# A head's row maxima: from a seven-row product on VectorE to one row by ScalarE and a DMA, with new ranks for the planner

## The chip, the cores and the metric

The kernel runs on one core of one Trainium2 chip. The metric is the device time of one execution in microseconds; several runs are taken and their median is given. A profiled execution of the same program gives the trace that is read here.

## The reference

Three layers follow one another. The first is causal attention with decay, for 4 batches of 8 heads, 576 positions, 64 columns a head. The other two are feed-forward layers on the 2304 tokens that come out of it, 512 columns wide.

```python
# attention, per batch and head; q, k, v: 576 x 64, f: 576
scores = q @ k.T / sqrt(64)
cum = cumsum(log(clip(f, 1e-4, 1)))
scores = where(causal, -1e9, scores + cum[:, None] - cum[None, :])
scores = scores - max(scores, axis=-1)
attn = exp(scores) / (sum(exp(scores)) + 1e-9)
x = attn @ v                                   # heads side by side: 2304 x 512
# second layer
x = ((x @ w_a) * (x @ w_b)) @ w_out            # 512 -> 1536 -> 512
# third layer
h = x @ w_in                                   # 512 -> 1024
s = h * softmax(h)
out = ((s - mean(s)) / sqrt(var(s) + 1e-6) * g_ln) @ w_out2    # 1024 -> 512
```

All tensors are float32 in HBM. The weights w_a, w_b, w_out, w_in and w_out2 are converted on the way in (`load_cols`), from 8-byte words.

## The kernel before, in words

**The planner.** The kernel does not issue instructions directly. Each piece of work is an `op` with an engine (or several to choose from), a rank (`key`), a cost in us, and the buffers it reads and writes. `Sched.run` then plays the whole program through once, when the kernel is built: at each step the engine and operation that could start first is taken, and among those of one engine that could start within `WIN` = 0.02 us of it the one with the lowest rank. The result is one fixed order of instructions for each engine. The dictionary `Y` holds the numbers from which ranks are made. The planner's costs stand in `t_act`, `t_dve`, `t_pool1`, `t_pool2` and `t_mm`; a DMA is done when earlier ones have passed at 230 GB/s, plus 2.0 us (lines 244 to 246):

```python
            if e == "SP":
                dma_free = max(dma_free, t + dur) + o.nbytes / 230.0e3
                done = dma_free + 2.0
```

All DMAs are issued by one queue, SP. Up to rank 210, where the plan leaves TensorE idle for more than 0.3 us, 70% of that gap is filled with small matmuls whose result nobody reads (line 1503, the filler).

**Precision.** A float32 matrix product is made of three products of reduced-precision parts: each operand has a high part (a cast) and a low part (the rest, a subtraction). That is why casts on ScalarE and subtractions on GpSimd or VectorE are everywhere.

**The attention.** A list of 40 jobs is worked off: the first half of 8 heads of batch 0 (256 positions, kind K0), their second half (320 positions, kind K1), and 24 whole heads (kind KF). Job j has the rank `Z[j]`: it starts at `Z0` and grows by `T0` for K0, `T1` for K1, `TA` for the first 8 KF heads and `TF` for the other 16. For each head: keys and queries are transposed on TensorE (`turn`, line 763) and split (`split_k`, `split_q`), a copy of each high part is moved to other partitions by a DMA (lines 776 and 790), and the running sums of log f come by DMA as two more rows (`load_cum`). Three sets of such buffers exist. Then follows:

- `max_scores`: a coarse product (line 820) whose row maxima VectorE takes tile by tile (lines 839 and 842). They stand in the columns of `mt`, 128 positions to a column; TensorE transposes that into PSUM (line 851), so that each of up to five rows holds the maxima of 128 positions.
- the spread: these maxima have to be subtracted inside the product of the scores. VectorE multiplies the transposed rows with a 0/1 mask, `bmask`, and writes seven rows of the buffer `MB` (line 863); for some K0 heads ScalarE does it instead, in two pieces (line 868). Against rows of -1 in `SB` the product then subtracts each maximum.
- `scores`: two products to a piece (lines 886 and 894); the second has 64 + 7 rows and contains sums and maxima.
- `exps`: the exponential on ScalarE (line 936), for KF heads the causal mask on GpSimd (945), the split into parts (952 and 958).
- `v_split` (972, 977), `weigh` (992) and `out_`: the product with v, and the division.

**The first product of the second layer.** After each half of a batch, `split_x` (1064, 1068) prepares its columns and 12 units follow (`up_unit`): 24 matmuls each (line 1082), one for each block of 128 columns of w_a and w_b. Their rank is `UK` above that of the unit. ScalarE and VectorE take the result (1101, 1103) and a DMA puts it into HBM. The columns of w_a and w_b are loaded and converted by `load_cols` (fetch at 594; 609, 618, 627, 629, 633; cast at 646; subtraction at 651), with ranks from `W0`, `WD0` and `WD1`. The batch-0 units need K0 heads (first half) or K1 heads (second half), and their weight columns.

**The rest.** w_out, w_in and w_out2 are loaded in the same way, into buffers that the attention no longer needs. `down` (1333) makes the second product of layer two, `expert` the third layer (1386 to 1476).

The functions that the change touches, and what calls them:

Of the kernel before, what the change touches and what calls it, by code (L numbers as in the profile page):

```python
# [24 lines left out]
def t_act(n, psum=False):  # L25
    return (0.155 if psum else 0.187) + n / 1200.0
# [41 lines left out]
class Sched:  # L68
# [223 lines left out]
    "WD0": 0.382,  # L292
    "WN": 4,
    "WD1": 4.394,
# [15 lines left out]
    "RA": 1,  # L310
    "TB": 1,
    "MM": 1,
    "MX": -0.17,
    "XK": -0.753,
# [5 lines left out]
def kernel(  # L320
# [16 lines left out]
    P = 128  # L337
# [40 lines left out]
    sml = pool.tile([P, 40], F32, name="sml")  # L378
# [177 lines left out]
    def load_cols(src_view, key, dst_hi, dst_lo, wbuf, wparts, tfetch=6.0, scale=None, kind=1,  # L556
                  after=(), places=False):
# [83 lines left out]

        def shaped(dst):
# [168 lines left out]
    def max_scores(t, st, K, key):  # L811

        ms = [s_.buf("att", bank_att(K.mb[i])) for i in range(len(K.mm))]

        def mm(part):
            for o, w, i, k0 in K.mm[part]:
                d0 = o + i * P - k0
                dw = min(P, o + w - d0)
                pm = K.pm and Y["MM"] and o <= d0 < o + w
# [8 lines left out]
        for part in range(len(K.mm)):  # L828
            more = [P for x in K.mm[part] if K.pm and Y["MM"] and x[3] <= x[2] * P < x[3] + x[1]]
            op((PE, t_mm([x[1] for x in K.mm[part]] + more)), key + 0.1 * part,  # L830
               lambda part=part: mm(part), r=[(CONST, "cmask"), (CONST, "identb"), (st, "kh"), (st, "qh"), (st, "cum0"), (st, "cum1"), (st, "rows")],
               w=[(ms[part], i) for _, _, i, _ in K.mm[part]])

        def red(part, o, w, i):
# [3 lines left out]
            if K.pm and Y["MM"]:  # L838
                nc.vector.tensor_reduce(
                    out=mt(st)[:n, 2 + i:3 + i], in_=x, op=ALU.max, axis=AX.X)  # L840
                return
            nc.vector.tensor_tensor_reduce(  # L842
                out=x, in0=x, in1=cmask[:n, off:off + w], scale=1.0, scalar=-3.0e38,
                op0=ALU.add, op1=ALU.max, accum_out=mt(st)[:n, 2 + i:3 + i])

        for j, (part, o, w, i) in enumerate(K.red):
            op(("DVE", t_dve(w) + (0.0 if K.pm and Y["MM"] else 0.14)), key + Y["MX"] + 0.3 + 0.3 * j,
# [23 lines left out]
        rw.fn = spread  # L871

    def scores(t, st, K, key):
# [4 lines left out]
        def mm(i, last):  # L878
            for c, pi, o, q0, q1 in K.pieces:
# [83 lines left out]
    def v_split(nb, K, key):  # L963
# [4 lines left out]
        def vv(part):  # L968
# [85 lines left out]
    def split_x(i, key):  # L1054
# [5 lines left out]
        for p in range(NP):  # L1060
# [3 lines left out]
            op(("ACT", t_act(n)), key + 0.3 * p, lambda p=p, s=src: nc.scalar.copy(  # L1064
                out=xsv(h, 0, n)[:, p], in_=s()), r=rd, w=[(xh, p)], after=AX1 if i == 1 else ())
# [486 lines left out]
```

## Time and profile before

| | us |
|---|---|
| median of 3 runs | 951.99 |
| lowest, highest | 948.39, 953.69 |
| the profiled execution, its time | 949.74 |
| the profiled execution, its span in the trace | 947.7 |
| TensorE busy | 916.3 |
| VectorE busy | 598.1 |
| ScalarE busy | 460.2 |
| GpSimd busy | 189.3 |

In the rows below, PE is TensorE, PEld its weight loads, DVE VectorE, ACT ScalarE, POOL GpSimd, and SP the queue that issues the DMAs. L863 is line 863 of the kernel. A group of instructions is given as line, engine, operation, output and input; then busy us and mean ns of one; then the idle time just before them and what ended it. A share or a sum of busy time is an average over stages with different limits, so the stages are to be read one by one. The filler counts as busy.

### The profile page before, as it was taken

The numbers are of one execution on the slowest core, as the hardware profiler recorded it, in microseconds if no ns is written. First come the engines' busy times: TensorE is split into PE (matmuls) and PEld (weight loads), VectorE is DVE, ScalarE is ACT, GpSimd is POOL, SyncE is SP. The second block draws the span as 40 slices with busy tenths as digits, with TensorE's granted clock in tenths as the row PEclk, the third lists the DMA queues.
The fourth block names the chain that finished last, engine by engine and source line by source line (L and its number), as shares of the span: only waits on it lengthen the run. The fifth ranks groups of instructions, "written<-read, shape, count | busy, mean of one in ns | idle before, by whom it ended". The sixth has DMA issues, their size and how long they took to land.

```text
span 947.7 us, 16069 instructions
## 1 busy us (share of the span) xinstructions
PE 916.3 (97%) x5888; PEld 835.8 (88%) x5888; DVE 598.1 (63%) x1162; ACT 460.2 (49%) x862; POOL 189.3 (20%) x280
## 2 busy tenths in 40 slices
PE   6789998999999999999999999999999999999997
PEld 5678997999999999999999889988888888888885
DVE  6799988777577766577454957744543444444553
ACT  3897877666555645445445645522322322232222
POOL 4122323444341332211211001110100010010100
PEclk8999999999999999999999999999999999999999
DMA  4656545334133423233226545412212121111000
GB/s 120 189 151 187 143 124 130 93 86 101 41 97 88 106 59 77 58 94 82 78 84 224 196 131 180 130 45 56 57 55 65 47 56 45 40 45 34 25 15 33
DMA packets 124001, 86.89 MB, mean 92 GB/s; under 512 B 74346, under 2 KB 114292, under 8 KB 123924
## 3 DMA queue, kind: packets, MB, share of 16 engines
q1 hardware_dynamic: 123924, 85.88, 32.3%
q8 instruction: 46, 0.75, 0.3%
q14 instruction: 31, 0.25, 0.1%
HBM read 56.86 MB, written 19.02 MB: 80 GB/s over the span
## 4 chain that ended last, share of the span: by engine, by line
PE 81%; DVE 2%; ACT 1%; issue 0%; POOL 0%; DVEq 0%; ACTq 0%
PE ps L1082 29%; PE ps L1333 16%; PE ps L1386 10%; PE ps L1463 10%; PE ps L992 7%; PE ps L894 2%; PE ps L820 2%; PE ps L886 2%; PE ps L1448 2%; PE ps L763 1%; DVE ps L842 0%; PE ps L851 0%; ACT pfw L936 0%; ACT pexp L952 0%; DVE wms L629 0%
## 5 line engine op out<-in xcount | busy, mean ns | idle before, releaser
L1082 PE MATMUL ps<-xs,wt 128*128 128x288 f32 (+2 forms) x2304 | 332.0, 298 | 0.6 <-ACT ats L1101 0.5
L1082 PEld LDWEIGHTS ps<-xs,wt 128*128 128x128 f32 x2304 | 312.9, 188 | 2.6 <-ACT ats L1101 0.7
L992 PE MATMUL ps<-pexp,VS 128*128 128x64 f32 (+5 forms) x600 | 96.8, 303 | 6.4 <-ACT pexp L952 3.3
L992 PEld LDWEIGHTS ps<-pexp,VS 128*128 128x128 f32 x600 | 90.5, 189 | 11.5 <-DVE pexp L958 3.5
L1463 PE MATMUL ps<-wt 128*128 128x512 f32 x408 | 98.2, 390 | 0.0
L1101 ACT COPY ats<-ps 128x288 f32<-128x288 f32 (+2 forms) x96 | 38.3, 399 | 117.4 <-PE ps L1082 113.8
L1333 PE MATMUL ps<-wt,sets 128*128 128x512 f32 (+1 forms) x420 | 92.7, 370 | 0.0
L1463 PEld LDWEIGHTS ps<-wt 128*128 128x128 f32 x408 | 76.0, 188 | 15.4
L1333 PEld LDWEIGHTS ps<-wt,sets 128*128 128x128 f32 x420 | 73.1, 188 | 12.9
L1325 POOL TENSOR_TENSOR wt<-nat,wt 128x512 fp32r<-128x512 f32 (+1 forms) x26 | 27.4, 1054 | 251.1 <-ACT wt L1321 251.1
L842 DVE CUSTOM_DVE_ANT_0 ps<-ps,cmask 128x512 f32<-128x512 f32 (+4 forms) x120 | 64.6, 551 | 11.5 <-PE ps L820 8.6
L1103 DVE TENSOR_TENSOR gts<-ps,ats 128x288 f32<-128x288 f32 (+2 forms) x84 | 38.3, 456 | 47.7 <-PE ps L1082 21.0
L945 POOL TENSOR_SCALAR_AFFINE_SELECT pfw<-pfw 128x128 f32<-128x128 f32 (+1 forms) x120 | 38.8, 351 | 139.4 <-ACT pfw L936 138.5
L1321 ACT CAST wt<-nat 128x512 fp32r<-128x512 f32 (+1 forms) x60 | 34.7, 579 | 55.1 <-PE ps L1333 26.4
L1386 PE MATMUL ps<-wt 128*128 128x512 f32 x240 | 57.8, 394 | 0.7 <-DVE wt L1346 0.7
L1403 ACT ACTIVATE xrw<-ps,sml 128x1024 f32<-128x1024 f32 x17 | 19.0, 1118 | 79.3 <-DVE sml L1401 79.3
L1454 DVE TENSOR_TENSOR wt<-ps,wt 128x512 fp32r<-128x512 f32 x34 | 23.3, 689 | 53.3 <-ACT wt L1451 53.3
L1401 DVE TENSOR_REDUCE sml<-ps 128x1 f32<-128x1024 f32 x18 | 22.0, 1225 | 49.2 <-PE ps L1386 49.2
L1386 PEld LDWEIGHTS ps<-wt 128*128 128x128 f32 x240 | 44.2, 188 | 9.9 <-DVE wt L1346 1.2
L894 PE MATMUL ps<-sets 71*128 71x448 f32 (+4 forms) x200 | 51.2, 332 | 0.0
L958 DVE TENSOR_TENSOR pexp<-pfw,pexp 128x960 fp32r<-128x960 f32 (+1 forms) x40 | 41.2, 1042 | 14.9 <-ACT pexp L952 14.8
L886 PE MATMUL ps<-sets 128*128 128x64 f32 (+5 forms) x200 | 49.7, 294 | 0.6 <-ACT pfw L936 0.5
(161 smaller groups left out, 1531.3 us busy)
## 6 DMA issues: line engine op xcount, KB each, us to landing
gs<-gts SPq DMA_DIRECT2D x60, 144.0 KB
sets<-sets SPq DMA_DIRECT2D x56, 144.0 KB
nat<-gs SPq DMA_DIRECT2D x36, 144.0 KB
raws<-in_moe_w_a_dram SPq DMA_DIRECT2D x10, 512.0 KB
pfw<-in_moe_w_b_dram SPq DMA_DIRECT2D x10, 512.0 KB
nat<-gs SPq DMA_DIRECT2D x36, 128.0 KB
out_dram<-xrw SPq DMA_DIRECT2D x18, 256.0 KB
nat<-in_k_dram SPq DMA_DIRECT2D x32, 128.0 KB
```

The source lines that it names most:

```text
L842: nc.vector.tensor_tensor_reduce(out=x, in0=x, in1=cmask[:n, off:off + w], scale=1.0, scalar=-3.0e38, op0=ALU.add, op1=ALU.max, accum_out= ...
L886: nc.tensor.matmul(dst, lhsT=SA(st)[:, ks], rhs=MA(st)[:, q0:q1], start=True, stop=False)
L894: nc.tensor.matmul(dst, lhsT=SB(st)[:D + NA, ks], rhs=MB(st)[:D + NA, q0:q1], start=False, stop=True)
L945: nc.gpsimd.affine_select(out=x, in_=x, pattern=[[1, w]], base=0, channel_multiplier=-1, compare_op=ALU.is_ge, fill=0.0)
L958: o.fn = lambda o=o, bh=bh, bl=bl, n=n, pf=pf: ENG[o.eng].tensor_tensor(out=pexp[:, 64 * bl.slot:64 * bl.slot + n], in0=pf(), in1=pexp[:, ...
L992: nc.tensor.matmul(bank(u, K.uo + q0, q1 - q0), lhsT=V[:, vp], rhs=src[:, o:o + q1 - q0], start=(k_ in K.first and ip == 0), stop=(k_ in K ...
L1082: nc.tensor.matmul(bank(u[m], 0, n_), lhsT=wv(m, wp, c)[:, kk], rhs=xsv(h, xx, n_)[:, kk], start=(n == 0), stop=(n == 3 * KD - 1))
L1101: op(("ACT", t_act(n_, True)), key - 50.0, lambda: nc.scalar.copy(out=atv(), in_=bank(u[0], 0, n_)), r=[(u[0], 0)], w=[(at, 0)])
L1103: op(("DVE", t_dve(n_)), key - 50.0, lambda: nc.vector.tensor_tensor(out=gtv(), in0=bank(u[1], 0, n_), in1=atv(), op=ALU.mult), r=[(u[1], ...
L1333: nc.tensor.matmul(bank(py, 512 * d, n), lhsT=WO[c][0][:, wp * DM:(wp + 1) * DM][:, ds_], rhs=ghv(gb, gp)[:, :n], start=(c == 0 and i == 0 ...
L1386: nc.tensor.matmul(bank(ph, half * 512, 512), lhsT=yv(yb, yp)[:, d, tsl], rhs=wi(d, wp)[:, fs], start=(n == 0), stop=(n == 3 * KD - 1))
L1463: nc.tensor.matmul(bank(po, 0, DM), lhsT=zp[:, c], rhs=w2(c, wp), start=(c == 0 and i == 0), stop=(c == NF2 - 1 and i == 2))
```

## The change

- `max_scores`: the maxima go into the columns 0 to 4 of `mt` (before: 2 to 6). After the transpose, ScalarE copies the five rows of PSUM into `MB`, partitions 96 to 100, and one DMA moves these rows, 512 bytes each, one behind another into the single row 66 of `MB`. Line 863's product and its ScalarE form are gone.
- `scores`: the second product has 64 + 3 rows.
- The casts of the high parts in `load_cols`, `v_split` and `split_x` can be done by GpSimd instead of ScalarE, whichever the planner finds done first (`HC` = 2).
- `raws`, `pfw`, `wms`, `ats` and `gts` become slices of one tile; `sml` is larger.
- A way to halve a maximum's columns is added to `red` and switched off (`HM` = 0). `load_cols` gets an argument `whole`, which no call sets. `YC` and `T2` are read by nothing. They are what is left of a scheme after Strassen, which this version does not use.
- Most numbers in `Y` are new, so the order of the instructions on every engine may be.

```diff
@@ Y
-    "Z0": 17.056,
-    "T0": 4.873,
-    "T1": 15.735,
-    "TA": 4.417,
-    "TF": 21.695,
-    "U0": 8.749,
+    "Z0": 16.046,
+    "T0": 5.412,
+    "T1": 7.324,
+    "TA": 8.365,
+    "TF": 20.381,
+    "U0": 0.0,
     "U1": 0.0,
-    "UF": 6.93,
+    "UF": 1.768,
     "UL": 1.453,
-    "LEAD": (1.3559648255683812, 1.1661755750630942),
-    "SHRINK": 1.832,
-    "W0": 0.0,
-    "WD0": 0.382,
+    "LEAD": (1.3991310183706258, 5.760862593817457),
+    "SHRINK": 0.0,
+    "W0": 45.348,
+    "WD0": 7.472,
     "WN": 4,
-    "WD1": 4.394,
+    "WD1": 0.318,
-    "BIAS": 0.48,
-    "UO": (8.320466715924777, 16.68815323789424, 17.92095945373172),
+    "BIAS": 0.176,
+    "UO": (7.480680559584226, 7.468926040897791, 8.302131475288967),
-    "UK": 87.852,
-    "L3": 6,
+    "UK": 328.111,
+    "L3": 9,
+    "HM": 0,
+    "HC": 2,
-    "MX": -0.17,
-    "XK": -0.753,
+    "MX": -8.098,
+    "XK": -5.566,
@@ load_cols; v_split and split_x likewise
-        op(("ACT", t_act(n)), key + 0.5, lambda: nc.scalar.copy(out=dst_hi, in_=shaped(dst_hi)),
-           r=[(wm, 0)], w=[(wbuf, (x, "h")) for x in wparts])
+        hc = op([("ACT", t_act(n)), ("POOL", t_pool1(n))][:Y["HC"]], key + 0.5, None,
+                r=[(wm, 0)], w=[(wbuf, (x, "h")) for x in wparts])
+        hc.fn = lambda: (nc.scalar.copy if hc.eng == "ACT" else nc.gpsimd.tensor_copy)(
+            out=dst_hi, in_=shaped(dst_hi))
@@ max_scores
-        rw = op([("DVE", t_dve((c1 - c0) * P)), ("ACT", (c1 - c0) * t_act(P, True))][
-            :2 if K is K0 and Y["RA"] else 1], key + 3.8, None,
-           r=[(ms[mp], "mT"), (CONST, "bmask")] + (PADS2 if K is not K0 else []), w=[(st, "rows")])
-
-        def spread():
-            x = MB(st)[D:D + NA, c0 * P:c1 * P].rearrange("p (c t) -> p c t", t=P)
-            m = bank(ms[mp], mo, P, NA)
-            if rw.eng == "DVE":
-                nc.vector.tensor_tensor(
-                    out=x, in0=m.unsqueeze(1).to_broadcast([NA, c1 - c0, P]),
-                    in1=bmask[:, c0:c1].unsqueeze(2).to_broadcast([NA, c1 - c0, P]), op=ALU.mult)
-            else:
-                for c in range(c0, c1):
-                    nc.scalar.activation(
-                        out=x[:, c - c0], in_=m, func=AF.Copy, scale=bmask[:, c:c + 1])
+        op(("ACT", t_act(P, True)), key + 3.8, lambda: nc.scalar.copy(
+            out=MB(st)[3 * 32:3 * 32 + NC, :P], in_=bank(ms[mp], mo, P, NC)),
+           r=[(ms[mp], "mT")], w=[(st, "rm")])
+        op(("SP", 0.54), key + 4.1, lambda: nc.sync.dma_start(
+            out=MB(st).bitcast(F32)[D + 2:D + 3, c0 * P:c1 * P],
+            in_=MB(st).bitcast(F32)[3 * 32 + c0:3 * 32 + c1, :P]),
+           r=[(st, "rm")] + (PADS2 if K is not K0 else []), w=[(st, "rows")], nbytes=512.0 * (c1 - c0))
@@ scores
-                        dst, lhsT=SB(st)[:D + NA, ks], rhs=MB(st)[:D + NA, q0:q1], start=False,
+                        dst, lhsT=SB(st)[:D + 3, ks], rhs=MB(st)[:D + 3, q0:q1], start=False,
                         stop=True)
```

## Rows read from the trace of the kernel before

**Rows 1.** The page: busy time by engine, and the chain that ended last.

```profile
PE 916.3 (97%) x5888; PEld 835.8 (88%) x5888; DVE 598.1 (63%) x1162; ACT 460.2 (49%) x862; POOL 189.3 (20%) x280
...
PE 81%; DVE 2%; ACT 1%; issue 0%; POOL 0%; DVEq 0%; ACTq 0%
```

**Rows 2.** Busy time by stage: stretch, its length, each engine's us (instructions), clock, DMA.

```profile
0.00:77.00 77.00, 57.48 (x481) 50.45 (x482) 60.74 (x121) 54.67 (x124) 23.18 (x53) 0.93 0.61 159
77.00:130.00 53.00, 52.23 (x420) 49.36 (x419) 48.24 (x81) 41.61 (x82) 11.97 (x10) 1.00 0.59 160
130.00:170.00 40.00, 35.70 (x294) 32.02 (x293) 35.78 (x75) 29.98 (x61) 15.12 (x21) 1.00 0.47 121
170.00:475.00 305.00, 304.42 (x2188) 298.49 (x2187) 208.24 (x420) 166.64 (x269) 93.32 (x155) 1.00 0.31 80
475.00:613.00 138.00, 137.74 (x931) 131.52 (x929) 91.41 (x158) 73.51 (x140) 17.00 (x14) 1.00 0.49 160
613.00:948.00 335.00, 328.75 (x1582) 274.00 (x1582) 153.65 (x310) 93.78 (x190) 28.70 (x27) 1.00 0.15 44
```

**Rows 3.** The same for line 1503 alone, with the sum.

```profile
0.00:77.00 77.00, 28.97 (x260) 24.04 (x260) 0.93 0.61 159
...
130.00:170.00 40.00, 10.13 (x105) 8.57 (x105) 1.00 0.47 121
...
sum 948.00, PE 40.68 PEld 33.44; mean PE 6.78 PEld 5.57
```

**Rows 4.** The same for line 1082 alone, second and third stage.

```profile
77.00:130.00 53.00, 31.29 (x228) 28.34 (x228) 1.00 0.59 160
130.00:170.00 40.00, 6.82 (x48) 6.10 (x48) 1.00 0.47 121
```

**Rows 5.** Groups on VectorE, 0 to 170 us, costliest first.

```profile
L839 DVE TENSOR_REDUCE mts<-ps 128x1 f32<-128x256 f32 (+4 forms) x40 | 20.5, 535 | 0.8 <-PE ps L824 0.5
...
L863 DVE TENSOR_TENSOR sets<-ps,bmask 7x384 fp32r<-7x384 f32 (+2 forms) x13 | 7.3, 558 | 1.9 <-PE ps L851 1.7
...
L842 DVE CUSTOM_DVE_ANT_0 ps<-ps,cmask 128x512 f32<-128x512 f32 (+4 forms) x11 | 6.1, 559 | 0.4 <-PE ps L820 0.3
...
L958 DVE TENSOR_TENSOR pexp<-pfw,pexp 128x960 fp32r<-128x960 f32 (+1 forms) x2 | 2.0, 992 | 0.8 <-ACT pexp L952 0.8
```

**Rows 6.** Groups on ScalarE, 0 to 170 us.

```profile
L646 ACT CAST wt<-wms 128x512 fp32r<-128x512 f32 (+1 forms) x18 | 9.5, 526 | 5.9 <-DVE wms L633 5.7
...
L646 ACT CAST wt<-pfw 128x512 fp32r<-128x512 f32 x10 | 6.2, 617 | 2.7 <-DVE pfw L633 2.7
...
L972 ACT CAST VS<-nat 128x640 fp32r<-128x640 f32 (+1 forms) x9 | 5.2, 573 | 0.0
...
L868 ACT ACTIVATE sets<-ps,bmask 7x128 fp32r<-7x128 f32 x10 | 3.0, 349 | 0.7 <-PE ps L851 0.6
```

**Rows 7.** What the DMA queue waited for, 900 to 948 us.

```profile
SPq L1547 <- DMA out_dram<-xrw: 1.5, 1, 1.5
```

**Rows 8.** Timeline of the DMA queue and TensorE: start, us, engine, line.

```profile
12.61 0.51 SPq L594 DMA_DIRECT2D pfw<-in_moe_w_b_dram  x1
...
13.70 1.14 SPq L804 DMA_DIRECT2D sets<-xs  x2
...
17.88 0.39 PE L820 MATMUL ps<-sets 66*128 66x256 f32 x1 [2.48 <-DMA sets<-xs]
...
944.31 0.33 SPq L1476 DMA_DIRECT2D out_dram<-xrw  x1
```

**Rows 9.** TensorE's waits from 170 us on, the longest: us, times, longest.

```profile
PE ps L1448 <- DVE pfw L1415: 0.9, 1, 0.9
```

**Rows 10.** Timeline of VectorE and GpSimd near 31 and 39 us.

```profile
31.55 0.42 DVE L627 TENSOR_SCALAR wms<-wms 128x512 f32<-128x512 f32 x1
...
38.75 1.29 POOL L651 TENSOR_TENSOR wt<-pfw,wt 128x512 fp32r<-128x512 f32 x1 [3.27 <-ACT wt L646]
...
39.28 1.04 DVE L627 TENSOR_SCALAR wms<-wms 128x512 f32<-128x512 f32 x1 [0.47 <-ACT wms L609]
```

More of the change, by code (lines that the diff above doesn't have):

```diff
@@ L377 @@
     gln = pool.tile([P, NF2], F32, name="gln")
-    sml = pool.tile([P, 40], F32, name="sml")
+    sml = pool.tile([P, 60], F32, name="sml")
     WW = 4 * KD * P
@@ L556, in load_cols @@
     def load_cols(src_view, key, dst_hi, dst_lo, wbuf, wparts, tfetch=6.0, scale=None, kind=1,
-                  after=(), places=False):
+                  after=(), places=False, whole=None):
         n = 256 if kind == 1 else 512
@@ L571, in load_cols @@
             at_raw = [(0, 16), (16, 16)] + ([(49, 16), (65, 16), (81, 16)] if places else [])
+            if whole is not None:
+                at_raw = [(0, 16), (16, 16), (81, 16)]
             raw = s_.buf("raw", lambda _: at_raw, "stage")
-            wm = s_.buf("wm", lambda _: [(32, 8), (41, 8)], "stage")
+            if whole is not None:
+                wm = whole
+            else:
+                wm = s_.buf("wm", lambda _: [(32, 8), (41, 8)], "stage")
         def stage(b, w):
@@ L640, in load_cols @@
                r=[(wm, 0), (CONST, "gln")], w=[(wm, 0)], port=True)
+        if whole is not None:
+            return wmv
         def shaped(dst):
@@ L813, in max_scores @@
         ms = [s_.buf("att", bank_att(K.mb[i])) for i in range(len(K.mm))]
+        halved = K is not K0 and t < Y["HM"]
+        masked = halved or (K.pm and Y["MM"])
         def mm(part):
@@ L828, in max_scores @@
         for part in range(len(K.mm)):
-            more = [P for x in K.mm[part] if K.pm and Y["MM"] and x[3] <= x[2] * P < x[3] + x[1]]
+            more = [P for x in K.mm[part] if masked and x[3] <= x[2] * P < x[3] + x[1]]
             op((PE, t_mm([x[1] for x in K.mm[part]] + more)), key + 0.1 * part,
-               lambda part=part: mm(part), r=[(CONST, "cmask"), (CONST, "identb"), (st, "kh"), (st, "qh"), (st, "cum0"), (st, "cum1"), (st, "rows")],
+               lambda part=part: mm(part), r=[(CONST, "cmask"), (CONST, "identb"), (st, "kh"), (st, "qh"), (st, "cum0"), (st, "cum1")],
                w=[(ms[part], i) for _, _, i, _ in K.mm[part]])
@@ L837, in red @@
             off = 4 * P - i * P
-            if K.pm and Y["MM"]:
+            if halved and w > P:
+                nc.vector.tensor_tensor_reduce(
+                    out=x[:, :w // 2], in0=x[:, :w // 2], in1=x[:, w // 2:], scale=1.0,
+                    scalar=-3.0e38, op0=ALU.max, op1=ALU.max, accum_out=mt(st)[:n, i:i + 1])
+                return
+            if masked:
                 nc.vector.tensor_reduce(
-                    out=mt(st)[:n, 2 + i:3 + i], in_=x, op=ALU.max, axis=AX.X)
+                    out=mt(st)[:n, i:i + 1], in_=x, op=ALU.max, axis=AX.X)
                 return
@@ L970, in vv @@
             return VSv[:, o:o + c1, part, 0::3]
-        op(("ACT", t_act(n)), key, lambda: nc.scalar.copy(
-            out=vv(0), in_=nat_of("v", nb, K)[:, :c1]),
-           r=all_nat(nb, K) + [(CONST, "vs0")], w=[(vb, 0)])
+        hc = op([("ACT", t_act(n)), ("POOL", t_pool1(n))][:Y["HC"]], key, None,
+                r=all_nat(nb, K) + [(CONST, "vs0")], w=[(vb, 0)])
+        hc.fn = lambda: (nc.scalar.copy if hc.eng == "ACT" else nc.gpsimd.tensor_copy)(
+            out=vv(0), in_=nat_of("v", nb, K)[:, :c1])
         o = op([("POOL", t_pool2(n)), ("DVE", t_dve(n))], key + 0.5, None,
@@ L1063, in split_x @@
             rd = [(xrb[b, p], (kq, 0)), (xrb[b, p], (kq, D))]
-            op(("ACT", t_act(n)), key + 0.3 * p, lambda p=p, s=src: nc.scalar.copy(
-                out=xsv(h, 0, n)[:, p], in_=s()), r=rd, w=[(xh, p)], after=AX1 if i == 1 else ())
+            hc = op([("ACT", t_act(n)), ("POOL", t_pool1(n))][:Y["HC"]], key + 0.3 * p, None, r=rd,
+                    w=[(xh, p)], after=AX1 if i == 1 else ())
+            hc.fn = lambda hc=hc, p=p, s=src: (
+                nc.scalar.copy if hc.eng == "ACT" else nc.gpsimd.tensor_copy)(
+                out=xsv(h, 0, n)[:, p], in_=s())
             o = op([("POOL", t_pool2(n)), ("DVE", t_dve(n))], key + 0.3 * p + 0.3, None,
```

18 lines of the change are left out of this document (8 added, 10 removed).

## The prediction

> **What bounds the kernel now.** I read the page first: TensorE is busy for 97% of the span and holds 81% of the chain that ended last [rows 1]. That looks as if nothing on VectorE could matter. The table by stage says where it is untrue. From 170 us on TensorE is full (304.42 of 305, then 137.74 of 138, then 328.75 of 335 with a tail of 6 us). Before 170 us it is busy 57.48 + 52.23 + 35.70 = 145.41 us, so idle for 24.6 [rows 2]. And not all of that is work: line 1503 is the filler which the kernel puts into the gaps its planner foresees, 40.68 us, all before 170 us, 28.97 of it before 77 us and 10.13 between 130 and 170 [rows 3]. So the first 170 us hold 24.6 + 40.7 = 65.3 us in which TensorE computes nothing, and the rest of the span is 916.3 - 40.7 = 875.6 us of work and 6.8 us of idle time. 65.3 + 875.6 + 6.8 = 947.7. The amount of real work does not change (the same matmuls; the last term of the scores has 67 rows in place of 71, and its columns, 448, 320 and so on, stay). So the forecast is a forecast of the 65.3.
>
> Who starves TensorE there? VectorE is busy 48.24 of 53 us between 77 and 130 us and 35.78 of 40 us after that, ScalarE 41.61 and 29.98 [rows 2]: VectorE is the nearer bound, with ScalarE some 15 points behind. Before 77 us neither is full (60.74 and 54.67): there the first heads' chain of waits, and fetches, set the pace. The up-projection starts at 77 us and is 31.3 us of TensorE's 53 in the second stage, but only 6.8 of 40 in the third [rows 4]: its first half of a batch (12 units of 24 matmuls) has used up the weight columns that were ready, and the second half waits for the last heads of the K1 kind. From 170 us it has a stock again and TensorE never lacks work.
>
> **The spread leaves VectorE.** Line 863 ran 13 times in the first 170 us, 7.3 us together, 0.56 each [rows 5]. The wider ones of the KF heads lie nearly all in stages where TensorE is full: taken at nothing, the cover is TensorE's own work (without it, some 0.8 us a head, 640 columns against the 0.56). Of the 7.3 us, what lies before 77 us frees an engine that was not full. I take 5 us off the 65.3, with 0 and 7.3 as ends.
>
> **The row by way of ScalarE and a DMA.** The new copy is one 128-column activation; the nearest row is line 868's, 349 ns [rows 6], 18 of them (two KF heads had got that far) replacing its 10 in the first 170 us: 2.8 us more on ScalarE, which has room. The transfer is new in this chain. Its bounds: the last store of the kernel, alone in its queue and 100 times larger, took 0.33 us to issue and kept SP waiting for 1.5 more [rows 7, 8]: 1.8 us. The other end is a pair of one-row transfers (line 804) issued at 13.70 us behind two 512 KB weight fetches, the second at 12.61: the matmul that needed the first of them started at 17.88, 4.2 us later [rows 8]. So a head's path grows by (0.35 + 1.8 to 4.2) - (0.4 to 0.8), or 1.4 to 4.1 us. Early on the queue is full of weight fetches, so I take 3 us. Behind the waiting issue on SP stand the next heads' loads and the copies of the up-projection's results; each is held back by at most the copy's wait, well below their slack, and SP's 0.5 us an issue, 16 times in 170 us, is 8 us of a queue that only issues. TensorE's scores of that head wait, and with fixed order all behind them. But three heads are in flight at a time. In the first wave nobody else has work for TensorE, so 3 us are lost once; with three sets the 8 K0 heads make 2.7 waves, 8 us at worst; at best nothing, when VectorE is late anyway. I take 3. After 170 us the planner has set the place of those scores 0.54 + 2.0 us behind the copy (lines 246 and the change), more than the 1.8 us of a free queue, and no TensorE wait after 170 us is longer than 0.9 us [rows 9]: nothing, with 24 heads times 1.6 us (4.2 - 2.6) as the price if the queue were always behind.
>
> **The new ranks** are the larger term. Ranks order what could start at the same time. By their sums the last K1 head moves from rank 166 (17.06 + 8 x 4.87 + 7 x 15.74) to 111 (16.05 + 8 x 5.41 + 7 x 7.32), and the last weight columns from about 190 to 89, while the first weights go from 0 to 45, behind most K0 heads. So both things that the third stage lacked come sooner: columns for the first half, and the K1 heads that open the second half, a stock of some 50 us (12 units, each a quarter wider than those of 24 x 31.29 / 228 = 3.3 us in [rows 4]). In the trace heads of the KF kind ran there instead: lines 842 and 958 with the KF tile have 6.1 + 2.0 us of VectorE before 170 us [rows 5], though their work could have waited. What the order can win is that stage's loss, 40 - 35.70 + 10.13 = 14.4 us. What it can spoil is the start of the up-projection. I take 10 of the 14.4; ends 0 and 14.4. In the late stages the higher key of the up-projection (87.9 to 328) only moves stock from the attention behind it: TensorE is full either way. Late next would be the weights of the second and third layers, which VectorE (91.41 of 138 us busy) has time for.
>
> **The casts that may go to GpSimd.** In the first 170 us lines 646 and 972 are 37 casts of 9.5 + 6.2 + 5.2 = 20.9 us on ScalarE [rows 6]; line 1064 has 8 smaller ones. Moved, they take work from an engine that is not the bound: 0 to 3 us gained. Against it: at 38.75 us GpSimd began a 1.29 us subtraction, and VectorE's clamp of a 512-column tile, begun at 39.28, took 1.04 us and ended at 40.32, 0.28 after GpSimd; the same clamp at 31.55 us took 0.42 [rows 10]. So a cast on GpSimd can cost VectorE up to 0.6 us. I guess that a quarter of the 37 move and a third of those block: 9 x 0.33 x 0.6 = 2 us, against 2 gained. Taken at 0; ends -3 and +22 (all 37 blocking).
>
> The merged working tile and the larger one for small values cost nothing: pieces of one tile are already used side by side (all banks are one tile) without waits on each other.
>
> **The sum.** 65.3 - 5 (spread) + 3 (transfer) - 10 (order) + 0 = 53.3, or 12 us less: a span of 935.7. The profiled execution took 949.74 us by the clock of the runs, 2.0 more than its span, and the median of the runs is 951.99, 2.3 above that. I scale the median: 951.99 x 935.7 / 947.7 = 940 us.
>
> **The rivals.**
> *The transfer takes the place of the spread* (no change). K0 and K1 heads become bound by three sets: 8 us for K0 and as much for K1 against 15 gained, about 951. For it: VectorE idles 16 us before 77 us, so latency does set the pace there. Against: between 77 and 130 us VectorE is 91% busy, and 3 us more per head on three sets is 1 us a head.
> *The ranks gain nothing and only the spread counts*: -5 + 3, 950. For it: with all engines choosing the earliest startable work, ranks decide little.
> *GpSimd blocks VectorE* (slower). 37 casts x 0.6 = 22 us of VectorE, minus the 12: about 962; it decides from 20 blocked casts up. For it: the pair of [rows 10]. Against: the largest group of VectorE's early work, line 839's 20.5 us, reads PSUM [rows 5] and doesn't touch what GpSimd touches, and GpSimd is under a third busy (23.18 of 77) [rows 2]. The Trainium skill (SBUF — State Buffer, Who interferes with whom) says that the port pair these two share is an exclusive lock held for the whole instruction. By that, the trace agrees: the clamp ended 0.28 us after GpSimd, not in proportion; and by the same rule every overlap costs its full remainder, 962 at worst.
> *Weights too late* (slower). If heads go first and at the opening of the up-projection more columns are missing than before, each missing one is a unit, 3.3 us of TensorE [rows 4]; seven missing are 23, 11 more than gained, so 963; it decides from four. Against: before 77 us VectorE has 16 idle us that weights can fill.
> *More than forecast*: the whole 14.4, the 7.3, and a transfer that hides: -21.7, 930.
>
> **Chances.** Forecast 0.46 (931 to 946), more than forecast 0.16, the transfer or the ranks leave it unchanged 0.22 together, blocked VectorE 0.09, late weights 0.07. About 0.5% (4.8 us) is what a measurement of this kernel tells from no change: the three runs spread over 5.3. Faster by over that 0.64, within 0.20, slower 0.16. The range leaves out a little of the best case (below 926) and about half of the slower ones (above 957): 926 to 957.
>
> **What would show it.** In the trace after: filler plus idle before TensorE fills up near 53 us; TensorE full from some 155 us on; VectorE's line for the spread gone; K1 heads done by 140 us; the longest TensorE wait on the row's transfer a few us, early only. Wrong would be: TensorE waits on that transfer repeated in the full stages; VectorE's clamps and shifts longer beside GpSimd's casts; a start of the up-projection clearly after 77 us; or waste that moved behind the attention, where the loads of the later layers would starve TensorE.

## The result and the profile after

The changed kernel took 959.38 us (median of 7 runs, 955.75 to 963.38) against 951.99 before: a ratio of 1.0083, 95% interval 1.0054 to 1.0112. By the ratio it is slower by about 7.9 us (the medians differ by 7.4); I forecast 940, faster by 12. The profiled execution took 958.55 us with a span of 956.8, 9.1 more than the 947.7 of before.

First the page of the changed kernel: busy time, the granted clock by slices of 24 us, and the chain that ended last.

```profile
PE 924.7 (97%) x5858; PEld 840.4 (88%) x5858; DVE 600.6 (63%) x1214; ACT 445.2 (47%) x842; POOL 117.1 (12%) x243
...
PEclk9899999899999999999999999999999999999999
...
PE 80%; DVE 3%; ACT 1%; DMA 1%; issue 1%; SPq 0%; DVEq 0%; ACTq 0%
```

The table by stage of the changed kernel answers to [rows 2] (stretch, its length, busy us of PE, PEld, DVE, ACT and POOL with counts, granted clock, DMA share, GB/s):

```profile
0.00:77.00 77.00, 61.55 (x458) 53.39 (x458) 54.73 (x114) 45.58 (x104) 20.66 (x56) 0.91 0.49 122
77.00:130.00 53.00, 47.99 (x391) 43.01 (x390) 47.51 (x84) 40.50 (x78) 10.24 (x12) 1.00 0.62 178
130.00:170.00 40.00, 36.86 (x293) 34.16 (x294) 33.39 (x77) 29.59 (x63) 9.95 (x15) 0.96 0.52 144
170.00:475.00 305.00, 302.59 (x2149) 295.51 (x2147) 204.96 (x437) 158.79 (x268) 60.77 (x138) 0.99 0.30 79
475.00:613.00 138.00, 138.00 (x932) 132.05 (x932) 90.45 (x164) 72.14 (x133) 7.32 (x13) 1.00 0.52 164
613.00:957.00 344.00, 337.73 (x1645) 282.24 (x1643) 169.56 (x340) 98.57 (x199) 8.11 (x10) 1.00 0.16 46
```

The filler alone (line 1516 now) answers to [rows 3], and the up-projection's units alone (line 1095), second and third stage, to [rows 4]:

```profile
0.00:77.00 77.00, 20.27 (x150) 15.19 (x150) 0.91 0.49 122
77.00:130.00 53.00, 10.40 (x100) 8.07 (x100) 1.00 0.62 178
```

```profile
77.00:130.00 53.00, 20.33 (x134) 17.12 (x134) 1.00 0.62 178
130.00:170.00 40.00, 15.31 (x95) 13.31 (x95) 0.96 0.52 144
```

Read it in three steps.

**The waste did not shrink, it moved.** I call idle time of TensorE plus filler the waste. Before 77 us it was 19.5 + 29.0 = 48.5 us and is now 15.4 + 20.3 = 35.7: 12.8 gained. Between 77 and 130 us it was 0.8 + 1.6 = 2.4 and is now 5.0 + 10.4 = 15.4: 13.0 lost. There the units had 31.29 us of TensorE [rows 4] and now have 20.33. From 130 to 182 us, with 10.1 and 9.7 us of filler, it is 14.4 and 14.5. Up to 182 us that makes 65.3 and 65.7. The last of these stretches, before and then after:

```profile
130.00:182.00 52.00, 47.70 (x380) 43.77 (x379) 43.55 (x96) 37.09 (x72) 19.53 (x28) 1.00 0.38 98
...
130.00:182.00 52.00, 47.10 (x346) 43.56 (x347) 40.66 (x93) 36.24 (x73) 13.31 (x22) 0.90 0.48 131
```

**The real work took longer.** Busy time less filler was 916.3 - 40.7 = 875.6 us and is 924.7 - 40.3 = 884.4, for the same matmuls. Most of it lies where the granted clock fell below full speed. These are the stretches of the changed kernel around them, and the two halves of the first 182 us (columns as above):

```profile
50.00:60.00 10.00, 8.41 (x56) 7.23 (x57) 6.95 (x13) 6.08 (x13) 3.71 (x5) 0.83 0.68 186
140.00:150.00 10.00, 9.98 (x73) 9.41 (x72) 6.86 (x13) 6.59 (x14) 2.45 (x3) 0.83 0.40 109
170.00:180.00 10.00, 8.24 (x45) 7.49 (x43) 5.76 (x12) 6.45 (x12) 1.80 (x6) 0.71 0.40 101
...
0.00:50.00 50.00, 37.19 (x271) 31.36 (x271) 32.70 (x75) 26.67 (x66) 13.17 (x47) 0.90 0.44 105
50.00:182.00 132.00, 119.46 (x921) 108.60 (x922) 110.20 (x215) 95.64 (x189) 31.03 (x44) 0.95 0.56 155
```

The kernel before was also at 0.90 up to 50 us, but at 1.00 from there to 182:

```profile
0.00:50.00 50.00, 34.94 (x288) 31.22 (x288) 34.62 (x71) 31.08 (x71) 15.18 (x44) 0.90 0.59 151
50.00:182.00 132.00, 122.47 (x992) 112.36 (x991) 117.92 (x228) 102.29 (x207) 39.49 (x47) 1.00 0.52 139
```

A mean of 0.95 over 132 us is 6.6 us of TensorE's time given away (the clock has two levels, 1.2 and 2.4 GHz). Some of that falls on idle time and filler. Counted in steps of 1 us over real work alone, 6.2 us were given away there, and before 50 us 2.9 against 2.6 in the kernel before: 6.6 more in all. So 0.4 of waste and 6.6 of clock stand for 7.0 of the 9.1 us; 2 us are not placed.

The clock also differs between executions of one program: of 103 executions of the kernel before that ran beside the experiments, the 20 with a mean clock of 0.994 or more took 950.0 us on average, the 9 with 0.987 or less 954.7. The seven of the changed kernel had 0.983 to 0.989, so 6.6 us is the reading of one pair of executions.

**What came ahead of a fall.** ScalarE's one copy of a row in this stretch, then SP's queue, then TensorE's timeline (start, length, idle time before it and its releaser), near 170 us of the changed kernel:

```profile
L874 ACT CAST sets<-ps x1: 254/254/254, 167.1 to 167.1; 5x128 fp32r<-5x128 f32 x1
```

```profile
167.17 0.66 SPq L753 DMA_DIRECT2D nat<-in_k_dram  x1
167.93 0.53 SPq L600 DMA_DIRECT2D fw<-in_moe_w_b_dram  x1
168.56 0.52 SPq L787 DMA_DIRECT2D sets<-sets  x1
169.17 0.54 SPq L749 DMA_DIRECT2D nat<-in_q_dram  x1
169.80 0.62 SPq L787 DMA_DIRECT2D sets<-sets  x1
170.51 0.77 SPq L877 DMA_DIRECT2D sets<-sets  x1
```

```profile
168.60 1.33 PE L1002 MATMUL ps<-pexp,VS 128*128 128x448 f32 x7 [0.21 <-DVE pexp L967]
...
173.29 0.47 PE L903 MATMUL ps<-sets 67*128 67x448 f32 x1 [1.36 <-DMA sets<-sets]
...
174.16 2.25 PE L1002 MATMUL ps<-pexp,VS 128*128 128x320 f32 x9
```

The row was ready at 167.35 us, was issued at 170.51 behind five other transfers, and its scores started at 173.29, 5.9 us after the copy. TensorE idled 1.36 us for it, and the narrower matmuls behind it ran at 250 ns each where wider ones had taken 190. The waits of TensorE in the changed kernel (us in all, times, longest) show how little of the loss is such waiting by itself:

```profile
PE ps L903 <- DMA sets<-sets: 4.2, 4, 1.8
PE ps L774 <- DMA nat<-in_q_dram: 2.7, 4, 1.5
PE ps L895 <- DVE pexp L967: 2.3, 1, 2.3
...
PE ps L1095 <- DVE wt L662: 1.4, 3, 0.8
```

The Trainium skill (TensorE: Matmul & The Clock Gate, HAM oscillation — how this bites in real kernels) says that a wait for a DMA between pieces of work can drop TensorE to the half clock, and that the price is then paid again each time. The trace agrees in part: the clock fell to 0.83, 0.83 and 0.71 in the three stretches above. The first and the last lie behind waits for the row's DMA (1.82 us until 50.94, 1.36 us until 173.29), the one near 140 us behind a wait of 2.28 us for VectorE (the line of `pexp`, until 138.35).

### The profile page after: what moved, and what is told of

It is laid out like the page before. It is cut to its first block, busy times and chain, and to the rows that moved or that the text cites. A ratio compares the mean times of both kernels' runs of the same rounds, so it can differ in the third digit from the quotient of the medians.

```text
span 956.8 us, 16094 instructions
## 1 busy us (share of the span) xinstructions
PE 924.7 (97%) x5858; PEld 840.4 (88%) x5858; DVE 600.6 (63%) x1214; ACT 445.2 (47%) x842; POOL 117.1 (12%) x243
## 4 chain that ended last, share of the span: by engine, by line
PE 80%; DVE 3%; ACT 1%; DMA 1%; issue 1%; SPq 0%; DVEq 0%; ACTq 0%
PE ps L1095 29%; PE ps L1346 16%; PE ps L1399 10%; PE ps L1476 10%; PE ps L1002 6%; PE ps L903 2%; PE ps L833 2%; PE ps L895 2%; PE ps L1461 2%; PE ps L774 1%; DVE pexp L967 0%; DVE sets L804 0%; DMA fw<-in_moe_w_b_dram 0%; DMA sets<-sets 0%; DMA nat<-in_k_dram 0%
## 5 line engine op out<-in xcount | busy, mean ns | idle before, releaser
L1095 PE MATMUL ps<-xs,wt 128*128 128x288 f32 (+2 forms) x2304 | 337.2, 300 | 3.4 <-DVE wt L662 1.4
L1002 PE MATMUL ps<-pexp,VS 128*128 128x64 f32 (+5 forms) x600 | 99.0, 309 | 2.6 <-DVE pexp L967 2.1
L1002 PEld LDWEIGHTS ps<-pexp,VS 128*128 128x128 f32 x600 | 93.6, 197 | 6.9 <-DVE pexp L967 2.2
L1476 PEld LDWEIGHTS ps<-wt 128*128 128x128 f32 x408 | 76.0, 188 | 15.4
L1114 ACT COPY fw<-ps 128x288 f32<-128x288 f32 (+2 forms) x96 | 38.3, 399 | 110.0 <-PE ps L1095 105.3
L1116 DVE TENSOR_TENSOR fw<-ps,fw 128x288 f32<-128x288 f32 (+2 forms) x84 | 38.2, 455 | 54.9 <-PE ps L1095 28.4
L1334 ACT CAST wt<-nat 128x512 fp32r<-128x512 f32 (+1 forms) x60 | 34.8, 579 | 48.5 <-PE ps L1346 34.3
L1338 DVE TENSOR_TENSOR wt<-nat,wt 128x512 fp32r<-128x512 f32 (+1 forms) x51 | 33.7, 662 | 35.8 <-PE ps L1461 26.1
L903 PE MATMUL ps<-sets 67*128 67x448 f32 (+4 forms) x200 | 51.8, 335 | 4.2 <-DMA sets<-sets 4.2
L954 POOL TENSOR_SCALAR_AFFINE_SELECT fw<-fw 128x128 f32<-128x128 f32 (+1 forms) x120 | 37.6, 342 | 146.8 <-ACT fw L945 143.9
L895 PE MATMUL ps<-sets 128*128 128x64 f32 (+5 forms) x200 | 50.8, 300 | 3.0 <-DVE pexp L967 2.3
L967 DVE TENSOR_TENSOR pexp<-fw,pexp 128x960 fp32r<-128x960 f32 (+1 forms) x44 | 43.8, 1007 | 13.4 <-ACT pexp L961 13.0
```

What stands on the lines that cost most here:

```text
L895: nc.tensor.matmul(dst, lhsT=SA(st)[:, ks], rhs=MA(st)[:, q0:q1], start=True, stop=False)
L903: nc.tensor.matmul(dst, lhsT=SB(st)[:D + 3, ks], rhs=MB(st)[:D + 3, q0:q1], start=False, stop=True)
L954: nc.gpsimd.affine_select(out=x, in_=x, pattern=[[1, w]], base=0, channel_multiplier=-1, compare_op=ALU.is_ge, fill=0.0)
L967: o.fn = lambda o=o, bh=bh, bl=bl, n=n, pf=pf: ENG[o.eng].tensor_tensor(out=pexp[:, 64 * bl.slot:64 * bl.slot + n], in0=pf(), in1=pexp[:, ...
L1002: nc.tensor.matmul(bank(u, K.uo + q0, q1 - q0), lhsT=V[:, vp], rhs=src[:, o:o + q1 - q0], start=(k_ in K.first and ip == 0), stop=(k_ in K ...
L1095: nc.tensor.matmul(bank(u[m], 0, n_), lhsT=wv(m, wp, c)[:, kk], rhs=xsv(h, xx, n_)[:, kk], start=(n == 0), stop=(n == 3 * KD - 1))
```

## The experiments

Two theories at first. Transfer: the row comes late, and gaps and clock follow. Order: the new ranks themselves cost, the transfer is hidden. A third, casts: GpSimd's casts hold up VectorE. Ratios are to the kernel before, run on the same chip beside each, with 95% intervals. "Order kept" means that each engine's list of work is that of the kernel named and one operation alone is exchanged; "order anew" means that the planner ran again.

**e1. The row's way alone, order of before kept.**

```
-  VectorE/ScalarE: MB[D:D+NA, c0*P:c1*P] = maxima x bmask
+  nc.scalar.copy(out=MB(st)[96:96 + NC, :P], in_=bank(ms[mp], mo, P, NC))
+  nc.sync.dma_start(out=MB(st)[D+2:D+3, c0*P:c1*P], in_=MB(st)[96+c0:96+c1, :P])
```

> The kernel before with its ranks and its order of all work kept, and one thing alone changed: at the place where VectorE (or, for some K0 heads, ScalarE) spread the maxima over seven rows, ScalarE copies five rows of 128 and SP moves them into one row; the scores' last term reads 67 rows. Transfer theory (the row comes late, TensorE gets gaps early and its clock falls there): slower than before by 5 to 9 us, 956 to 961. Order theory (the new ranks cost it, the transfer is hidden): 949 to 953, since 0.56 us a head leave VectorE and 1.8 to 2.6 us of transfer come in. Cast theory (GpSimd): the same 949 to 953.

Measured: 981.96 us, 1.0319 (1.0298 to 1.0341). TensorE's waits for the row, first up to 170 us, then from there on:

```profile
PE ps L888 <- DMA sets<-sets: 17.7, 12, 6.5
...
PE ps L888 <- DMA sets<-sets: 8.2, 12, 1.4
```

An order that keeps no time for the transfer pays 26 us of waiting, 30 in all: far more than I expected of either theory. This transfer is hidden where its place is planned, and not because it is small.

**e2. The spread back on VectorE, e3. the row not awaited, e4. the casts back on ScalarE; order of the changed kernel kept.**

```
e2 -  nc.scalar.copy(...); nc.sync.dma_start(...)     # the row
   +  nc.vector.tensor_tensor(out=MB[D:D+NA, ...], in0=maxima, in1=bmask, op=mult)
e3 -  out=MB(st)[D + 2:D + 3, ...]
   +  out=MB(st)[D + 3:D + 4, ...]                    # nobody reads it
   -  memset(SB[D:D+NA], -1.0)
   +  memset(SB[D:D+NA], -30.0)                       # the row that is read holds a constant
e4 -  nc.scalar.copy if hc.eng == "ACT" else nc.gpsimd.tensor_copy
   +  nc.scalar.copy
```

> The changed kernel with its order of all work kept, but at the place of ScalarE's copy VectorE spreads the maxima over seven rows as before, and nothing is sent. Transfer theory: 949 to 953, the loss of 7 us is gone. Order theory: 957 to 963, since the order is the same and VectorE's places have no hole for the 0.56 us a head. Cast theory: 957 to 963 too.

> The changed kernel with every instruction in its place, but the transfer writes a row that nobody reads (partition 67), so that the scores don't wait for it; the row that they read holds a constant, -30 by 1, so this leaves out the subtraction of the maxima. Transfer theory, the wait by itself: 949 to 953, and the four waits of TensorE for it (4.2 us in sum) are gone, and with them the two stretches at a low granted clock near 140 and 175 us. If the queue of SP and not the wait were the cost: 956 to 959. Order and cast theories: 956 to 959.

> The changed kernel with its order kept, but each cast that its planner gave to GpSimd is run by ScalarE at the same place of the order. Cast theory (a cast on GpSimd of 0.43 to 0.70 us is slower than ScalarE's and holds up VectorE): 949 to 954. Transfer and order theories: 957 to 963, since ScalarE's places have no hole for some 21 casts of 0.25 to 0.5 us.

Measured: e2 956.80 us, 1.0048 (1.0032 to 1.0065); e3 957.32, 1.0056 (1.0038 to 1.0075); e4 959.97, 1.0096 (1.0063 to 1.0129). e3 leaves out the subtraction of the maxima, so only its time counts. Without the transfer or without its wait the new order is still about 5 us slower than before. So the transfer is worth some 2.6 to 3.3 us of the 7.9 (the intervals of both overlap with that of the changed kernel, 1.0054 to 1.0112, so the size is loose), and neither of the two runs did what the transfer theory wanted. In e3 TensorE no longer waits for the row, yet the granted clock still fell near 175 us (0.77 from 170 to 180), and from 50 to 182 us it was lower than with that wait:

```profile
50.00:182.00 132.00, 121.52 (x910) 110.94 (x911) 109.47 (x212) 94.84 (x188) 30.52 (x44) 0.91 0.56 154
```

So the waits for the row are not what the clock hangs on, or not they alone. e2 had the clock at 0.99 there and no more waste up to 182 us (64.1) and was slow all the same: 2.4 us more of idle time behind 182 us are found, the rest of its loss is not placed. That casts on GpSimd cost anything is not shown: taking them back gains nothing (the interval of e4 is 6 us wide).

**e5 and e6. More filler, each kernel's order kept.** The filler's limit of 210 is a time of the plan in us, not a rank.

```
-    "FG": 0.3, "FF": 0.7,
+    "FG": 0.1, "FF": 1.0,
```

> The changed kernel with the same order, but its filler takes the whole of each gap that the planner foresees before 210 us, from 0.1 us up, in place of 0.7 of those from 0.3 us up. Clock theory (of the 7 us lost, most is real work that ran at half the clock in the stretches near 51, 140 and 175 us, after TensorE had idled): those stretches go, 951 to 955. Order theory (the waste stands between 77 and 130 us because weight columns are late, whatever the clock): 957 to 962, since filler only takes the place of idle time.

> The kernel before with the same more eager filler. Its clock fell only before 42 us, 11 us in sum. Clock theory: 946 to 951, a part of some 5 us. Otherwise 951 to 955, filler that runs over into the work.

Measured: e5 (the changed kernel) 955.66 us, 1.0037 (1.0022 to 1.0051); e6 (before) 949.68, 0.9972 (0.9961 to 0.9982). The stretch of e5 that answers to the 0.95 above:

```profile
50.00:182.00 132.00, 125.16 (x1077) 117.41 (x1077) 114.70 (x226) 96.49 (x191) 32.06 (x45) 1.00 0.57 155
```

The clock held at 1.00 and 4.4 us came back (0.46%): the clock has a share in the loss. The profiled execution is the fastest of e5's twelve, but the mean clock was 0.991 to 0.996 in all twelve. In the profiled executions the waste rose by 6.3 us, to 72.0, while the real work fell from 884.4 to 872.0, of which the clock, counted as above, accounts for 6.8. But both kernels gain by more filler, and 0.65% stays between them.

**e7 to e12. Ranks, way and casts set separately, order anew each time.** The edits are values of Y and the choice of engines:

```
e7   before + the new Y                       e8   changed kernel + the old Y, "HC": 2
e9   e8 + "FG": 0.1, "FF": 1.0                e10  e8 + "HC": 1       (casts on ScalarE)
e11  before + casts may go to GpSimd          e12  e8 + "W0": 45.348, "WD0": 7.472, "WD1": 0.318
```

> The kernel before with the new ranks alone, its order made anew from them: the spread stays on VectorE (or, for K0, ScalarE), casts stay on ScalarE. The step of the prediction (the ranks bring the K1 heads and the last weight columns forward, worth 10 us by themselves): 940 to 948. Theory that the ranks only suit the operations that they were chosen with: 958 to 968, with waste of more than 70 us before 170 us.

> The changed kernel with the ranks of before, its order made anew: the row goes by ScalarE and a DMA whose time the planner knows, casts may go to GpSimd. Theory that the new ranks are what costs: 945 to 951. Transfer theory (a planned transfer still loses to what the queue does): 955 to 965, with several waits of TensorE for the row before 170 us.

> The changed kernel with the ranks of before, as in the run of that name, and the eager filler on top. Clock theory: its clock fell as long as that of before, so the same 3 us come off, 944 to 947.5. If filler and clock had nothing more to give: 948.5 to 951.

> The changed kernel with the ranks of before and all casts on ScalarE, its order made anew: the way of the row alone. Theory that the way of the row by itself is worth its 2 us: 948 to 951. Theory that the casts on GpSimd make room on ScalarE for the copy and are what paid: 953 to 960.

> The kernel before with its ranks and its spread, but casts may go to GpSimd, its order made anew. Theory that the way of the row pays: 951 to 955. Theory that the casts pay: 947 to 950. Blocked VectorE (the rival of the prediction): 957 and more.

> The changed kernel with the ranks of before except the three of the weight columns (first at 45 in place of 0, later ones closer together). Theory that the late weights are what the new ranks cost: 957 to 965, with filler and idle time between 77 and 130 us of 10 us and more against 4 or 5 with the old ones. If the heads' ranks are the cost: 948 to 952.

Measured: e7 971.64 us, 1.0196 (1.0174 to 1.0219); e8 949.15, 0.9970 (0.9957 to 0.9983); e9 950.27, 0.9975 (0.9962 to 0.9988); e10 961.11, 1.0092 (1.0072 to 1.0112); e11 957.93, 1.0056 (1.0036 to 1.0075); e12 971.74, 1.0191 (1.0166 to 1.0215). With way and casts in, the new ranks cost 1.0083 / 0.9970, 1.1% or 10.8 us; without them 2.0%, 19 us. That is the term for which I had taken 10 us off. The filler of e9 gave nothing more: the old ranks' clock falls early, where much of what runs slowly is filler. In e8 the second stage has little waste; in e12, which differs by the three ranks of the weight columns alone, it has as much as the changed kernel. For each, the stage and its filler alone, e8 first:

```profile
77.00:130.00 53.00, 52.01 (x436) 49.53 (x434) 45.90 (x81) 34.97 (x73) 19.30 (x20) 1.00 0.54 152
...
77.00:130.00 53.00, 3.95 (x42) 3.43 (x42) 1.00 0.54 152
```

```profile
77.00:130.00 53.00, 48.60 (x406) 43.64 (x404) 47.90 (x76) 34.60 (x67) 21.33 (x19) 1.00 0.66 179
...
77.00:130.00 53.00, 12.12 (x123) 10.00 (x124) 1.00 0.66 179
```

1.0 + 4.0 us of waste against 4.4 + 12.1. (e12 computes something else than the reference, for a reason that is not known, so it is a support and no proof.) But e10 and e11 are a warning: the way alone and the casts alone, each planned anew, lose 9 and 5 us, and both together gain 3. An order made anew carries a scatter of several us that is no price of an operation. e11's time lies where its expectation had put a blocked VectorE, but VectorE's clamps of 512 columns took 466 and 429 ns there (means of its two groups up to 182 us) against 513 and 527 in the kernel before, so it is not that.

**e13 to e16. Is it scatter, or the late weight columns?** Three sets of ranks from small random variations, chosen for the shortest plan, two near the old ones and one near the new ones; and the new ranks of the heads alone.

```
e13  e8, "W0": 0.468, "WD0": 0.373, "WD1": 4.393, "T1": 16.116, "MX": -3.186, ...
e14  e8, "W0": 0.481, "WD0": 0.0, "WD1": 4.682, "T1": 16.072, ...
e15  changed kernel, "W0": 40.802, "WD0": 9.514, "WD1": 0.016, "T1": 7.167, ...
e16  e8, with Z0, T0, T1, TA, TF, LEAD and SHRINK of the changed kernel
```

> The changed kernel with a set of ranks near those of before (first weight column at 0.5), found by small random variations and chosen as the shortest plan of some thousands. Theory that early weights are the good property: 943 to 949, waste between 77 and 130 us of at most 6 us. Theory of scatter between orders: anywhere from 947 to 962.

> As the run beside it, another such set near the ranks of before (first weight column at 0.1). Early weights good: 943 to 950. Scatter: 947 to 962.

> The changed kernel with a set of ranks near its own (first weight column at 40.8), found and chosen in the same way; its plan is as short as those of the two runs beside it. Theory that late weights are the bad property: 953 to 962, with 12 us of waste and more between 77 and 130 us and a clock that falls after 50 us. Scatter: 945 to 960, with no order among the three.

> The changed kernel with the ranks of before except those of the heads (K1 heads 7.3 apart in place of 15.7, and what goes with them). Theory that the weights' ranks are the cost and the heads' the gain that I forecast: 943 to 950. Theory that each set of ranks only fits as a whole: 958 to 970, with heads in front of the weight columns again starving the up-projection.

Measured: e13 947.18 us, 0.9956 (0.9940 to 0.9973); e14 946.93, 0.9956 (0.9939 to 0.9973); e15 953.75, 1.0019 (1.0001 to 1.0037); e16 970.92, 1.0212 (1.0189 to 1.0236). e13 and e14 beat both kernels. (The first weight column of e14 has rank 0.5, not the 0.1 of its expectation.) The grouping is that of the property: the late-weight set is 6.6 us behind. But these are three sets, and other ranks differ between them too. The first 182 us of e13, then of e15:

```profile
50.00:182.00 132.00, 124.37 (x981) 113.04 (x981) 110.84 (x216) 97.60 (x201) 50.54 (x65) 1.00 0.54 142
```

```profile
50.00:182.00 132.00, 121.46 (x928) 111.06 (x929) 115.99 (x226) 92.92 (x185) 31.65 (x44) 0.95 0.56 151
```

e16 says that early columns are not enough: the heads' ranks, set to the new values without the rest, lose 20 us, and not between 77 and 130 us.

**e17 and e18. Whose gain is that of e13 and e14?** e17 gives the kernel before the same search; e18 is e14 with its order kept and e2's edit.

> The kernel before, nothing of the change in it, with ranks found by the same search near its own. If the 4 us that e13 and e14 took off come from the search and not from the way of the row and the casts: 946 to 949. If they come from these: 950 to 953.

> The kernel of e14 with its order kept and the spread back on VectorE at the place of ScalarE's copy, nothing sent. If the way of the row pays where the order suits it: 949 to 955. If it is worth nothing or the transfer costs more than it saves, as in the new order (e2): 943 to 947.

Measured: e17 949.18 us, 0.9972 (0.9956 to 0.9987); e18 951.51, 0.9992 (0.9980 to 1.0004). So most of the gain is the search's; what way and casts add, some 0.16%, lies within the intervals. In e14's order the row's way is worth 0.36%, 3.4 us, clear of the intervals; in the changed kernel's it cost 3.3, which is not clear of them: one operation, and most likely two signs, by the order around it. (In both, VectorE has the spread at a place that keeps no room for it, which flatters the way of the row.)

The runs in one table, worked out from the tables by stretch as idle time plus filler of TensorE (us), with the granted clock from 50 to 182 us and the median's ratio. Waste and clock are those of one profiled execution each:

| kernel | columns from | 0-77 | 77-130 | 130-182 | sum | clock 50-182 | ratio |
|---|---|---|---|---|---|---|---|
| before | 0 | 48.5 | 2.4 | 14.4 | 65.3 | 1.00 | 1 |
| e17 | 1.4 | 49.3 | 2.4 | 14.2 | 65.8 | 1.00 | 0.9972 |
| e8 | 0 | 50.9 | 4.9 | 9.5 | 65.3 | 1.00 | 0.9970 |
| e13 | 0.5 | 48.0 | 2.0 | 11.1 | 61.1 | 1.00 | 0.9956 |
| e14 | 0.5 | 51.0 | 4.0 | 8.8 | 63.8 | 1.00 | 0.9956 |
| e18 | 0.5 | 51.9 | 4.2 | 10.6 | 66.7 | 0.99 | 0.9992 |
| e10 | 0 | 50.8 | 4.6 | 15.0 | 70.4 | 1.00 | 1.0092 |
| e11 | 0 | 48.4 | 5.6 | 16.7 | 70.6 | 0.96 | 1.0056 |
| e16 | 0 | 53.9 | 4.5 | 14.3 | 72.6 | 0.97 | 1.0212 |
| after | 45.3 | 35.7 | 15.4 | 14.5 | 65.7 | 0.95 | 1.0083 |
| e2 | 45.3 | 34.7 | 15.1 | 14.4 | 64.1 | 0.99 | 1.0048 |
| e3 | 45.3 | 37.9 | 13.3 | 15.1 | 66.4 | 0.91 | 1.0056 |
| e4 | 45.3 | 36.2 | 14.1 | 17.0 | 67.3 | 0.92 | 1.0096 |
| e15 | 40.8 | 37.6 | 12.8 | 13.9 | 64.3 | 0.95 | 1.0019 |
| e7 | 45.3 | 34.0 | 18.3 | 18.8 | 71.1 | 0.99 | 1.0196 |
| e12 | 45.3 | 41.2 | 16.5 | 18.5 | 76.3 | 0.95 | 1.0191 |

In all of these, columns from 0 to 1.4 go with 2 to 6 us of waste in the second stage, columns from 40 on with 13 to 18. (e1, not in the table, has columns from 0 and 11.0 us there, among its many waits for the row.) The sums say less: in after, e2, e3, e4 and e15 they are near that of before, since what the second stage loses was won ahead of it. Late columns move the waste; the price shows in the clock, which from 50 us on is below 1.00 in every kernel of the table with late columns, but also in e11, e16 and e18. The table ends at 182 us. Over the whole span, idle time and filler are 72.1 us in before, 80.3 in e10 and 89.4 in e16: 8.3 of the 11.6 us and 17.3 of the 23.3 us by which the spans of these two are longer.

## Why the prediction was wrong

**The place** was read rightly: the loss arises before 182 us. **The bound** was not: I had called VectorE the nearer one, but its freed time bought nothing (busy 151.5 of the first 180 us before, 141.4 after, with TensorE's waste the same). That the chains of waits set the pace instead is what remains, and is argued, not shown.

**The new ranks (-10) is the step that failed.** I wrote that both things which the third stage lacked come sooner, columns and the last K1 heads, and priced that stage's 14.4 us alone. The stage still wastes 14.5. The heads did come sooner before 77 us, worth 12.8, but the columns were moved behind them, and I took their *last* rank (190 to 89) for what matters, though their *first* one went from 0 to 45: the stock that carried the up-projection through the second stage was gone, worth 13.0. With way and casts kept, the ranks cost 10.8 us (e8 against after): the waste up to 182 us is nearly the same (65.3 and 65.7), the real work is not (875.2 and 884.4), and 7.7 us of that difference is work at the half clock, counted in the same steps of 1 us. My rival "weights too late" had the right place and the wrong sign to look for: the units did not start later, they started at 66.8 us instead of 77.6 and then ran slower, 20.3 us of them in the second stage for 31.3. That it was the columns is borne out by e8 and e12, whose second stages waste 4.9 and 16.5 us.

**A term was missing.** I took the real work as constant. At the half clock it is not: 6.6 us more than before, 4.4 given back by filler in e5 (before gains 2.7 by the same filler). Where the clock falls matters: in the first 50 us of before 5.1 us of clock were given away, 2.6 of them over real work; between 50 and 182 us of the changed kernel 6.8, of them 6.2 over real work.

**The spread and the transfer (-5 + 3).** The -2 is of the size that the runs show, with either sign: -3.4 in e14's order, +2.6 to +3.3 in the changed kernel's. With casts and old ranks it is -2.9 (e8). The longest wait for the row is 1.8 us, within the few that I named, but one of 1.4 us came at 173 us, where I had allowed nothing; the 5.9 us from copy to scores is above my 4.2, more than half of it SP's queue. My bound for a queue that is always behind, 24 waits of 1.6 us after 170 us, was 38 us; e1 had 24 waits and 26 us, but half of the waits and 17.7 us before 170. The copy took 254 ns, not 349.

**The casts (0)** hold as far as e4 can tell. Of the 37 casts 15 went to GpSimd up to 182 us, not 9, with those of `split_x` 21. VectorE's clamp of 512 columns beside them, as a group of the changed kernel (count, busy us, mean ns, idle time before it):

```profile
L633 DVE TENSOR_SCALAR fw<-fw 128x512 f32<-128x512 f32 x20 | 8.3, 420 | 2.8 <-ACT fw L615 2.6
```

At 420 ns the clamp is as short as the undisturbed one [rows 10], so the rival of a blocked VectorE falls. The rule of the exclusive lock that I cited (the Trainium skill, SBUF — State Buffer, Who interferes with whom) is not contradicted; no run here shows it set the time. The pair of [rows 10] supports it less than I said: a clamp that is held up until GpSimd ends should then take its 0.42 us, and it ended 0.28 us later.

**The signs I named:** waste near 53 us (it is 65.7), TensorE full from 155 us (from 182), K1 heads done by 140 (true, the last of their reductions ends at 133.6).

What stays open: 2 us of after's 9.1 and most of e2's loss, why some waits of TensorE are followed by the half clock and others are not, and why the orders of e10 and e16 leave TensorE without work for so much longer.

## What to carry to other kernels

A set of ranks chosen for one kernel is no improvement that can be priced by itself: ask of each rank that moves what it is moved behind and which stock that empties, and add up the waste over all stages, not in the one that looked worst. Where an order is fixed by a plan, judge a new operation by exchanging it with the order kept, and again with ranks chosen anew for both versions; a single new plan on either side can hide 3 us behind 10 of scatter. Where TensorE must wait, let it wait early or under filler: here idle pieces among real work were followed, near 51, 140 and 174 us, by real work at the half clock.

## What the runs showed of the hardware

The half clock can follow gaps that look harmless. In the changed kernel TensorE waited 1.82 us for a row near 50 us, and then five transposes took 1.27 us that had taken 0.73 some ten us earlier. TensorE's timeline of the changed kernel:

```profile
42.19 0.73 PE L774 MATMUL ps<-ident,nat 128*128 128x128 f32 x5
...
50.94 0.39 PE L903 MATMUL ps<-sets 67*128 67x256 f32 x1 [1.82 <-DMA sets<-sets]
...
51.78 1.27 PE L774 MATMUL ps<-ident,nat 128*128 128x128 f32 x5
```

Not every such gap is followed by it. In the kernel before TensorE waited 1.87 us in the same part of the run, and the granted clock was 1.00 from 40 to 60 us:

```profile
45.21 0.28 PE L851 MATMUL ps<-ident,mts 128*7 128x128 f32 x1 [1.87 <-DVE mts L839]
```

In e5 the wait of 2.28 us for `pexp` is still there (until 136.82), with more filler ahead of it (27 matmuls in place of 19), and the clock stayed at 1.00.

In the changed kernel a transfer of one row of 2.5 KB inside SBUF took 2.8 us from its issue to the matmul that needed it (170.51 to 173.29), and waited longer than that, 3.2 us, for its turn in SP's queue.
